# The last token group of a fused attention and expert kernel: 12 of 20 blocks take their first product from seven half-size products

## The chip, the core and the metric

The kernel runs on one core of a Trainium2 chip. The core has a matrix engine (TensorE, PE in the profile; PEld is its weight loads), a vector engine (VectorE, DVE), a scalar engine (ScalarE, ACT), GpSimd (POOL), SyncE (SP), and DMA engines that move data between the device memory and the core's own memory. The engines run side by side, each in the order of its own instructions, and wait for each other through semaphores. Matmul results land in PSUM, a small memory of banks of 512 numbers in each of 128 partitions. The metric is the device time of one execution in microseconds (us); lower is better.

## The reference

A sketched polynomial attention makes `x` (4352 tokens of 128 numbers); a routing then balances a matrix `P` of token and expert weights in eight rounds; eight experts with one hidden layer of 1024 each are summed with these weights:

```python
    logits = x @ w_gate
    logits = logits - logits.max()
    P = np.exp(logits)
    for _ in range(8):
        P /= P.sum(1, keepdims=True) + 1e-09
        P /= P.sum(0, keepdims=True) + 1e-09
        P *= N / E
    for e in range(E):
        h = np.maximum(x @ w1[e], 0.0)
        ye = h @ w2[e]
        out += P[:, e:e + 1] * ye
```

N is 4352, D 128, E 8 and F 1024, all float32.

## The kernel before, in words

Tokens lie along the free dimension, so a first product takes 128 features in and gives 128 hidden units out for some hundred tokens. A list `groups` (line 767) cuts the work into groups of tokens with the experts that each of them meets; an item is a group with one expert, and a block is a part of an item's hidden units.

- Nine plain groups without routing weights run in and between the attention and the routing, since they don't need `P`. Function `steps` (line 1654) yields their blocks in pieces, and `fill` (line 1746) drops these pieces between the statements of `attention` (line 635) and of `routing` (line 702). `passed` counts the pieces, and `aside` holds other small jobs that are due at a count of pieces.
- Five groups of three times 256 tokens follow (`middle`, line 1330). There both products are formed from fewer products of half or quarter size, at the price of sums on DVE, ACT and by accumulating DMAs. The matrix engine is addressed there as four tiles of 64 rows by 64 columns, which run at once. The order of every instruction is written out by hand (`SEAM`, `DRAIN` and the like).
- The last group has 2 times 256 tokens and the experts 3 to 7: five items of four blocks, 20 blocks in all, again out of `steps`. I number them 0 to 19. The first steps of blocks 0 to 2 are already issued inside `middle`. In a block, four steps each form 128 hidden units for 256 tokens (`first`, line 1173: two matmuls side by side, each on all 128 rows and one half of the columns, then a relu on ACT). The second product is formed from seven half-size products instead of eight (`seven`, line 1260; two side by side again), for which `two` (line 1187) makes sums of the hidden units on DVE, and `sums_of_two` (line 193) makes four sums of the parts of W2 for each expert, each 128 x 256, on DVE, in the last group itself. Second products stand `LAG` = 8 steps behind their first products.
- Both kinds of items need x times the routing weight: `prepare_x` (line 864) loads a broadcast row of `P` (tile `px`), `weigh_by_vector` (line 809) multiplies it by x. In the five middle groups `weigh_half` (880), `copy_half` (893) and `join_halves` (900) make the sums of x: a scaled half, a copy of it, and four accumulating DMAs on POOL's queue, of which the third reads what the first two wrote.
- In the routing every round has a reduction over experts (line 731), one over tokens (line 738), a pair of small matmuls that add over partitions (line 742) and the scaling of both (lines 735 and 748). DVE does all but the matmuls; these stand at a fixed place in PE's order, so PE waits there if DVE is late.
- During the same time `forms_ahead` (line 276) makes the first weights' sums for the experts 1 to 7 with DMAs on SP's and POOL's queues and sign changes on ACT (line 295), and stores them in device memory; `forms_of_five` (line 626) sets when.

The matrix engine works on float32 in two passes, so each matmul of the program shows as two records in the trace.

Of the kernel before, what the change touches and what calls it, by code (L numbers as in the profile page):

```python
# [44 lines left out]
def kernel(  # L45
# [12 lines left out]
    nc = tc.nc  # L58
# [558 lines left out]
    def forms_at(e, area, *steps_):  # L617
        for at_, do in zip(steps_, forms_ahead(e, area)):
            aside.setdefault(passed[0] + at_, []).append(do)

    def forms_of_two():
        kx = pieces(ld.tile([P, SA, D], F32, tag="k", name="kx", bufs=1), 2)
# [79 lines left out]
    def routing():  # L702

        forms_of_five()
        yield 6
        logits(0)
        logits(1)
        yield 0.5
        logits_turned()
        logits(2)  # L710
        yield 0.5
        logits_turned()
        logits_turned()
# [12 lines left out]

        step = 1.5 * 2.0 ** (23 - 149 + 64)
        nc.vector.tensor_scalar(pw[:, :, 0:E], pw[:, :, 0:E], step, step, op0=Alu.add, op1=Alu.subtract)
        for it in range(ITERS):
            rs = sk.tile([P, SA], F32, tag="rs", name="rs")  # L730
            nc.vector.reduce_sum(rs, pw, axis=AX.X)
            nc.vector.reciprocal(rs, rs)
            yield 1.25
            p1 = p1s[it % 2]
            nc.vector.scalar_tensor_tensor(p1[:, 0:SA], rs.unsqueeze(2).to_broadcast([P, SA, E]), UP,
                                           pw[:, :, 0:E], op0=Alu.mult, op1=Alu.mult)
            cs = sk.tile([P, E], F32, tag="cs", name="cs")
            nc.vector.reduce_sum(cs, p1.rearrange("p g e -> p e g"), axis=AX.X)
            yield 3
            pc = bank()[:, 0:E]  # L740
            for s in range(2):
                nc.tensor.matmul(pc[64 * s:64 * (s + 1)], ones[:, 0:64], cs, start=True, stop=True,  # L742
                                 tile_position=(0, 64 * s))
            cr = sk.tile([P, E], F32, tag="cr", name="cr")
            nc.vector.reciprocal(cr, pc)
# [382 lines left out]

    blocks = [(j, q) for j in range(len(items)) for q in range(FO // (4 if tiles_of(j) == 3 else 2))]
    LAG, given = 8, []

    HELD = 8
    hs = {}

    def room_of(k):

        lo, n, t, _, weighted = groups[items[blocks[k][0]][0]]
        if t == 3:  # L1140
            if "x" not in hs:
                hs["x"] = pools[0].tile([P, 25, NT3], F32, name="hx", bufs=1)
            return hs["x"] if k % 2 == 0 else hb[:, 0:25 * NT3].rearrange("p (b n) -> p b n", n=NT3)
        base = hs["x"].rearrange("p b n -> p (b n)") if weighted else hb
        size = 4 * (NT3 if weighted else 480)
        one, other = (13 * NT3 + size * (k % 3), size * (k % 2)) if weighted else (size * (k % 3), size * (3 + k % 2))

        m = k - held_blocks[0]
# [38 lines left out]
    def two(k):  # L1187
# [5 lines left out]
        def step(c):  # L1193
            if k == 0:
                c = 2 * (c % 2) + c // 2
            f, t = 2 * q + c // 2, c % 2
            first(k, f, t * n, (t + 1) * n, h[c], k % 2)

        def less(out, a, b):
# [60 lines left out]
    def seven(k):  # L1260
# [2 lines left out]
        _, w2, ws = loaded_w[j]  # L1263
        h, ts, _ = hs[k]
        lo, hi = slice(0, H2), slice(H2, DM)
        p1 = (w2[:, 2 * q, lo], h[0], 0, 0, 0)

        five, six = (0, 2) if weighted_of(k) else (2, 0)
        p6 = (ws[:, 1, q], ts[2], six, 1, 0)
        p2 = (w2[:, 2 * q + 1, lo], h[2], 1, 0, 0)  # L1270
        p4 = (w2[:, 2 * q + 1, hi], ts[3], 1, 1, 0)
# [382 lines left out]
    def steps():  # L1654
# [13 lines left out]
        for k in ks:  # L1668
            if k in news:
                if k == news[0]:  # L1670
                    while todo or sums_at:
                        between(t)
                        t += 1
                    phase.append(True)
                    yield 0
                    middle()
                    yield 0
                continue
            if k == len(blocks):
                for i, ps in enumerate(last_products()):  # L1680
                    todo.setdefault(t + i, []).extend(ps)
            if k < len(blocks):
# [25 lines left out]
                m, step, sums_ = ready.get(k) or two(k)  # L1708
                products = eight if g in DIRECT else seven
            for c in range(m if k < len(blocks) else 4):  # L1710
                if k < len(blocks) and k not in ready:
                    step(c)
                between(t)
                if k < len(blocks) and first_new - 2 <= j < first_new:
                    for do, *a in TAIL.get(16 * (j - first_new + 2) + 4 * q + c, ()):
# [3 lines left out]
                if k < len(blocks) and c == 0:  # L1719
# [2 lines left out]
                            sums_at.setdefault(t + i, []).append(lambda i=i, f=sums_: f(i))  # L1722
                    if k < len(blocks) - 2 and k not in held_blocks:
                        for i, ps in enumerate(products(k)):
                            todo.setdefault(t + LAG + i, []).extend((k, p) for p in ps)
                share = n / 480 * (16 / 15 if g in DIRECT else 1)
                if k >= len(blocks):
                    while later:
                        later.pop(0)()
                elif later and (c % 2 or share > 0.9 or c and weighted):  # L1730
                    later.pop(0)()
                if k not in ready:
                    yield share
# [119 lines left out]
```

## Time and profile before

| | |
|---|---|
| runs | 882.81 us (median of 3; 882.0 to 884.62) |
| the profiled execution's own time | 883.17 us |
| its span on the core | 881.4 us |
| granted TensorE clock | 0.999 of full speed |
| PE busy / DVE busy / ACT busy | 874.2 / 790.9 / 570.6 us |

The profile's page lists for each engine how long it was busy, a map of the span in 40 slices, and the chain of work that ended last. Other views give the busy time of each engine in chosen stretches, the single instructions in order of time, the instructions grouped by line, and who waited for whom. In a row such as `64*64 64x256 f32` the first part is the rows and columns of the matrix engine that are active, and the second the moving operand. A busy PE is a modelled figure, since matmuls overlap; the distances between starts are measured.

### The profile page before, as it was taken

The numbers are of one execution on the slowest core, as the hardware profiler recorded it, in microseconds if no ns is written. First come the engines' busy times: TensorE is split into PE (matmuls) and PEld (weight loads), VectorE is DVE, ScalarE is ACT, GpSimd is POOL, SyncE is SP. The second block draws the span as 40 slices with busy tenths as digits, with TensorE's granted clock in tenths as the row PEclk, the third lists the DMA queues.
The fourth block names the chain that finished last, engine by engine and source line by source line (L and its number), as shares of the span: only waits on it lengthen the run. The fifth ranks groups of instructions, "written<-read, shape, count | busy, mean of one in ns | idle before, by whom it ended". The sixth has DMA issues, their size and how long they took to land.

```text
span 881.4 us, 28702 instructions
## 1 busy us (share of the span) xinstructions
PE 874.2 (99%) x11790; PEld 652.2 (74%) x11790; DVE 790.9 (90%) x1631; ACT 570.6 (65%) x1308; POOL 176.6 (20%) x244
## 2 busy tenths in 40 slices
PE   9999999999999999999999999999999999999997
PEld 6787567564777888887878778788777777776665
DVE  7679689888999999999999999999998999998875
ACT  3346578668676677667676766666766766665643
POOL 2131433121212121312132112221222122200000
PEclk9999999999999999999999999999999999999999
DMA  8999699575887887777786776697577777674340
GB/s 238 282 287 291 150 232 230 140 175 186 233 217 214 215 252 213 211 196 212 220 209 178 212 217 176 176 245 226 156 179 222 216 217 186 203 204 97 96 105 13
DMA packets 97459, 174.64 MB, mean 198 GB/s; under 512 B 29088, under 2 KB 68848, under 8 KB 92480
## 3 DMA queue, kind: packets, MB, share of 16 engines
q1 hardware_dynamic: 74904, 139.65, 50.1%
q0 software_dynamic: 21264, 33.00, 21.6%
q8 instruction: 93, 1.52, 0.7%
q10 hardware_dynamic: 1160, 0.15, 0.1%
q14 instruction: 38, 0.31, 0.1%
HBM read 125.67 MB, written 25.08 MB: 171 GB/s over the span
## 4 chain that ended last, share of the span: by engine, by line
PE 98%; DMA 1%; DVE 0%; ACT 0%; issue 0%; SPq 0%; DVEq 0%; ACTq 0%
PE s L1634 42%; PE a L1347 38%; PE a L1179 14%; PE a L430 1%; PE a L556 1%; DMA qx<-in_q_dram 1%; PE s L462 0%; PE a L397 0%; PE a L520 0%; PE s L482 0%; PE a L482 0%; ACT hb L1183 0%; PE a L742 0%; SPq L156 0%; PE a L597 0%
## 5 line engine op out<-in xcount | busy, mean ns | idle before, releaser
L1347 PE MATMUL a<-xe,w 64*64 64x384 f32 x2164 | 417.2, 483 | 0.0
L1634 PE MATMUL s<-hb,ws 64*64 64x256 f32 (+4 forms) x2962 | 382.6, 384 | 0.0
L1634 PE MATMUL s<-hx,ws 64*64 64x256 f32 (+1 forms) x2894 | 348.9, 376 | 0.0
L1347 PE MATMUL a<-de,w 64*64 64x384 f32 x1600 | 307.3, 483 | 0.0
L1634 PEld LDWEIGHTS s<-hb,ws 64*64 64x64 f32 (+1 forms) x2962 | 203.5, 133 | 62.7 <-issue 16.6
L1634 PEld LDWEIGHTS s<-hx,ws 64*64 64x64 f32 (+1 forms) x2894 | 196.2, 133 | 55.2 <-issue 12.5
L1249 DVE TENSOR_TENSOR hb<-hb 128x512 f32<-128x512 f32 (+1 forms) x340 | 187.4, 576 | 1.4 <-ACT hb L1382 1.1
L1347 PEld LDWEIGHTS a<-xe,w 64*64 64x64 f32 x2164 | 145.7, 133 | 18.6 <-issue 1.1
L1382 ACT ACTIVATE hx<-a 128x384 f32<-128x384 f32 x204 | 97.0, 492 | 63.0 <-PE a L1347 61.5
L1382 ACT ACTIVATE hb<-a 128x384 f32<-128x384 f32 x204 | 97.7, 492 | 58.9 <-PE a L1347 57.5
L1179 PE MATMUL a<-xT,w 128*64 128x256 f32 (+3 forms) x576 | 129.8, 454 | 0.1
L1347 PEld LDWEIGHTS a<-de,w 64*64 64x64 f32 x1600 | 110.6, 133 | 17.3 <-ACT hb L1382 0.6
L1249 DVE TENSOR_TENSOR hx<-hx 128x512 f32<-128x512 f32 (+1 forms) x204 | 118.1, 594 | 0.0
L905 POOL DMA_DIRECT2D de<-xe x68 | 57.1, 989 | 295.2 <-ACT de L898 175.3
L1183 ACT ACTIVATE hb<-a 128x256 f32<-128x256 f32 (+3 forms) x148 | 66.9, 454 | 54.8 <-PE a L1179 49.3
L1378 ACT ACTIVATE hb<-a 128x384 f32<-128x384 f32 x136 | 66.7, 491 | 32.7 <-PE a L1347 31.8
L1387 DVE TENSOR_TENSOR a<-a,hb 128x384 f32<-128x384 f32 x136 | 76.6, 563 | 10.0 <-PE a L1347 5.9
L1376 ACT COPY a<-a 128x384 f32<-128x384 f32 x136 | 63.0, 464 | 32.5 <-PE a L1347 31.9
L1179 PEld LDWEIGHTS a<-xT,w 128*64 128x64 f32 x576 | 57.9, 137 | 24.2 <-issue 3.5
L1200 DVE TENSOR_TENSOR hb<-hb 128x416 f32<-128x416 f32 (+7 forms) x90 | 59.7, 664 | 14.4 <-ACT hb L1183 10.2
L1634 PE MATMUL s<-hb,w 128*64 128x256 f32 (+3 forms) x280 | 68.8, 434 | 0.0
L905 POOL DMA_DIRECT2D de<-de x34 | 29.7, 872 | 131.3 <-issue 74.3
(227 smaller groups left out, 1016.9 us busy)
## 6 DMA issues: line engine op xcount, KB each, us to landing
ws<-ws SPq DMA_DIRECT2D x34, 1280.0 KB, 6.6
w<-wl SPq DMA_DIRECT2D x34, 512.0 KB, 8.0
w<-wf SPq DMA_DIRECT2D x33, 512.0 KB, 8.6
px<-pT SPq DMA_DIRECT2D x34, 384.0 KB, 9.5
w<-in_moe_w_dram SPq DMA_DIRECT2D x16, 512.0 KB, 4.3
de<-xe POOLq DMA_DIRECT2D x34, 192.0 KB, 3.2
de<-de POOLq DMA_DIRECT2D x34, 192.0 KB, 8.2
ws<-in_moe_w_dram SPq DMA_DIRECT2D x7, 512.0 KB, 7.6
```

Source lines behind the costliest of these rows:

```text
L430: nc.tensor.matmul(pv[64 * s:64 * (s + 1), i], kp[0:n, H * t + h].rearrange("p i j -> p (i j)"), vx[0:n, slots[h], t, :], start=(t == 0 an ...
L905: tc.keep_in_program_order(nc.gpsimd.dma_start(out=out, in_=x, accum_op=Alu.add))
L1179: nc.tensor.matmul(ph[sl], loaded_w[j][0][:, P * f + H2 * s:P * f + H2 * (s + 1)], sources[j][:, lo:hi], start=True, stop=True, tile_posit ...
L1183: last_relu[:] = [nc.scalar.activation(out=out, in_=ph, func=Act.Relu).ins.name]
L1200: nc.vector.tensor_tensor(out, a, b, op=Alu.subtract)
L1249: nc.vector.tensor_tensor(places(out), places(a), places(b), op=Alu.subtract if off else Alu.add)
L1347: nc.tensor.matmul(out[sl], w[r, c0 + H2 * s:c0 + H2 * (s + 1)], x[r], start=start, stop=stop, tile_position=(H2 * row, H2 * s), skip_grou ...
L1376: witness(k, p, 1, nc.scalar.copy(b, bx))
L1378: witness(k, p, 5, nc.scalar.activation(out=m5s[p], in_=b, func=Act.Copy, scale=1.0 if p else -1.0))
L1382: ins = nc.scalar.activation(out=out, in_=x, func=Act.Relu)
L1387: ins = nc.vector.tensor_tensor(by if what == 1 else raw(k, p, 1, 1), bb[p], m5s[p], op=Alu.add)
L1634: mm = nc.tensor.matmul(sums[g][i][H2 * s:H2 * (s + 1), n * place:n * (place + 1)], w, x, start=c == (2 if t == 3 and row is None else 1) ...
```

## The change

Blocks 6 to 17 of the last group (`MIXED`) no longer form their first product by four steps. They go in pairs, and for each of the two blocks seven half-size products stand in for it (`mixed_product`): each is two matmuls in tiles of 64 rows by 64 columns, so that four matmuls run at once. A pair takes seven slots (`mixed_slot`), and each slot also issues ACT's and DVE's work on the results: relus, a seeded copy (`seed`), a sign change (`turned_five`), sums (`plus_five`) and the sums for the second products. Products number 4 of a pair run in the first two slots of the next pair; after the last pair they run in two slots of their own beside block 18. Second products, which stay on all 128 rows, stand between the slots.

For these blocks x needs sums as in the middle groups: `mixed_weigh` or `mixed_turn`, `mixed_copy`, and `mixed_join` with its four accumulating DMAs, at the places that `AHEAD` sets. The items of the experts 4 to 7 load `W2`, both stored forms of `W1` and the stored sums of `W2`, and experts 4 and 7 `W1` as well (`mixed_weights`); before they loaded `W1` and `W2`.

The sums of `W2` for the experts 4 to 7 are no longer made in the last group but during the routing (`pairs_ahead`): for each a load of `W2` (512 KB, SP), four DVE sums and a store (512 KB, SP).

```diff
+    def sums_of_pairs(e, w2, ws):
+        def load():
+            tc.keep_in_program_order(nc.sync.dma_start(out=w2, in_=moe_w2[e].rearrange("(fo fi) d -> fi fo d", fi=P)))
...
+        def some(i):
+            o, a, b, op = sums_[i]
+            return lambda: nc.vector.tensor_tensor(o, a, b, op=op)
+        def keep_():
+            stored_pairs[e] = dram.tile([P, 4, FO // 2, H2], F32, name=f"ws2{e}")
+            tc.keep_in_program_order(nc.sync.dma_start(out=stored_pairs[e], in_=ws))
+        return load, *(some(i) for i in range(4)), keep_
+    def pairs_ahead():
...
+        for n, e in enumerate(range(4, E)):
+            at_ = passed[0] + 15 + 9 * n
+            for later_, do in zip((0, 6, 7, 7, 8, 8), sums_of_pairs(e, w2, ws)):
+                aside.setdefault(at_ + later_, []).append(do)
@@ routing @@
         forms_of_five()
+        pairs_ahead()
         yield 6
@@ prepare_w @@
+        elif j in mixed_items:
+            mixed_weights(j)
@@ new, beside two and seven @@
+    mixed_items = range(len(items) - 4, len(items))
+    MIXED = range(len(blocks) - 14, len(blocks) - 2)
+    def mixed_join(j):
+        xe, de = mixed_x[j]
+        for out, x in ((de[upper], xe[lower]), (de[lower, 1], xe[upper, 1]), (de[:, 0], de[:, 1]),
+                       (xe[lower, 1], xe[lower, 0])):
+            tc.keep_in_program_order(nc.gpsimd.dma_start(out=out, in_=x, accum_op=Alu.add))
+    def mixed_product(pair, p, n):
...
+        out, row, w, c0, x, start, stop = {
+            1: (bx, 0, wl, fa, xe[:, 0], not p, False), 2: (bx, 1, wl, fa, xe[:, 0], False, True),
+            3: (by, 1, wl, fb, de[:, 0], False, True), 4: (b, 1, wf, fb, xe[:, 1], False, True),
+            5: (by, p, wf, fa, de[:, 1], not p, True), 6: (b, 0, wf, fb, de[:, 0], False, True),
+            7: (b, 0, wl, fb, xe[:, 1], False, True)}[n]
+        for s in range(2):
+            sl = slice(H2 * s, H2 * (s + 1))
+            mm = nc.tensor.matmul(out[sl], w[r, c0 + H2 * s:c0 + H2 * (s + 1)], x[r], start=start, stop=stop,
+                                  tile_position=(H2 * row, H2 * s), skip_group_check=True)
...
+    ROW_SLOTS = (((0, 5), (0, 4)), ((0, 1), (1, 4)), ((1, 1), (1, 5)), ((0, 6), (0, 2)), ((1, 6), (1, 2)),
+                 ((0, 7), (0, 3)), ((1, 7), (1, 3)))
+    def mixed_slot(k, w):
...
+        for row, (p, n) in enumerate(ROW_SLOTS[w % 7] if w < 7 else ()):
+            pair = before if row and w < 2 else now
+            if pair:
+                mixed_product(pair, p, n)
...
+    AHEAD = {(2, 0): (fetch_x(J5),), (3, 0): (turn_to(J4, 0, 0),), (3, 1): (turn_to(J4, 0, 1),),
+             (3, 2): (turn_to(J4, 1, 0),), (3, 3): (turn_to(J4, 1, 1), join(J4)),
+             (5, 0): (weigh(J5, 0),), (5, 1): (copy_of(J5, 0),), (5, 2): (weigh(J5, 1),),
+             (5, 3): (copy_of(J5, 1), join(J5)), (6, 0): (fetch_x(J6),),
+             (8, 0): (fetch_x(J7), lambda: prepare_w(J6)), (8, 3): (weigh(J6, 0),), (8, 4): (weigh(J6, 1),),
+             (8, 5): (copy_of(J6, 0),), (8, 6): (copy_of(J6, 1), join(J6)),
...
+             (12, 4): (turn_to(J7, 1, 1), join(J7))}
@@ steps @@
+            if k in MIXED:
+                if (k - MIXED[0]) % 2:
+                    continue
+                for c in range(7):
+                    mixed_slot(k, c)
+                    if c == 0:
+                        ends = [seven(k + s) for s in range(2)]
...
+                        for i, ps in enumerate(ps if ps[5] else (*ps[:4], [], ps[4])):
+                            todo.setdefault(t + 10 + i, []).extend((k, p) for p in ps)
+                    ahead_of(k, c)
+                    between(t)
...
+                    t += 1
+                    yield 1
+                continue
...
+                tail = 4 * (k - len(blocks) + 2) + c
+                if 0 <= tail < 4:
+                    mixed_slot(None, tail)
```

The first number in a key of `AHEAD` is the block of the last group (0 to 19), the second the step or slot in it; J4 to J7 are the items of the experts 4 to 7.

More of the change, by code (lines that the diff above doesn't have):

```diff
@@ new lines, in mixed_rooms, with mixed_weigh @@
+    def mixed_rooms(j):
+        mixed_x[j] = [pools[0].tile([P, 2, HALF], F32, tag=tag, name=tag, bufs=3)[:, :, 0:NT3] for tag in ("xe", "de")]
+        return mixed_x[j]
+    def mixed_weigh(j, i):
+        xe = (mixed_x.get(j) or mixed_rooms(j))[0]
+        sl = slice(NT3 * i, NT3 * (i + 1))
+        x, pb = xT[:, groups[items[j][0]][0]:][:, sl], sources[j][:, sl]
+        if i:
+            nc.vector.scalar_tensor_tensor(xe[:, i], x, -1.0, pb, op0=Alu.mult, op1=Alu.mult)
+        else:
+            nc.vector.tensor_tensor(xe[:, i], x, pb, op=Alu.mult)
@@ new lines, with mixed_pair @@
+    m5_rooms = [hb[:, NT3 * (32 + p):NT3 * (33 + p)] for p in range(2)]
+    side, beside = [], {}
+    def mixed_pair(k):
+        if not beside:
+            a, b = ([t[:, NT3 * p:NT3 * (p + 1)] for p in range(2)] for t in (bank(), bank()))
+            beside["bx"], beside["by"] = [b[0], a[1]], [a[0], b[1]]
+            beside["b"] = [bank()[:, 0:NT3] for _ in range(2)]
+        i = (k - MIXED[0]) // 2 % 2
+        h = hb[:, NT3 * (16 + 8 * i):NT3 * (24 + 8 * i)].rearrange("p (a b n) -> p a b n", a=2, b=4)
+        t = hs["x"][:, 8 * i:8 * (i + 1)].rearrange("p (a b) n -> p a b n", a=2)
+        hv, tv = ([x[:, :, c] for c in range(4)] for x in (h, t))
+        if k >= len(blocks) - HELD:
+            x = hb[:, 2 * NT3 * (k - len(blocks) + HELD):][:, 0:4 * NT3].rearrange("p (a b n) -> p a b n", a=2, b=2)
+            hv[2], tv[3] = x[:, :, 0], x[:, :, 1]
+        for s in range(2):
+            hs[k + s] = ([x[:, s] for x in hv], [x[:, s] for x in tv], (h[:, s, 1::2], h[:, s, 0:2], t[:, s, 0:2]))
+        return k, hv, tv
@@ new lines, in mixed_product @@
+    def mixed_product(pair, p, n):
+        k = pair[0] + p
+        j, q = blocks[k]
+        (wl, wf), (xe, de) = mixed_w[j], mixed_x[j]
+        fa = P * (4 * (q // 2) + p)
+        fb = fa + 2 * P
+        bx, by, b = (beside[x][p] for x in ("bx", "by", "b"))
+        out, row, w, c0, x, start, stop = {
[3 more added lines that the diff above has]
+            7: (b, 0, wl, fb, xe[:, 1], False, True)}[n]
+        r = (lower, upper)[row]
+        for s in range(2):
+            sl = slice(H2 * s, H2 * (s + 1))
+            mm = nc.tensor.matmul(out[sl], w[r, c0 + H2 * s:c0 + H2 * (s + 1)], x[r], start=start, stop=stop,
+                                  tile_position=(H2 * row, H2 * s), skip_group_check=True)
+            if not s and (n, p) in ((1, 0), (5, 1)) and (n, p) in seen_by:
+                tc.add_manual_dep(mm.ins, seen_by.pop((n, p)), SYNC, reason="row tiles of one bank")
@@ L1134, with ahead_of @@
+    def ahead_of(k, c):
+        for do in AHEAD.get((k - len(blocks) + 20, c), ()):
+            do()
     HELD = 8
@@ L1146, in room_of @@
         one, other = (13 * NT3 + size * (k % 3), size * (k % 2)) if weighted else (size * (k % 3), size * (3 + k % 2))
+        if k >= len(blocks) - 2:
+            one = 16 * NT3 + size * (k % 2)
         m = k - held_blocks[0]
@@ L1729, in steps @@
                         later.pop(0)()
-                elif later and (c % 2 or share > 0.9 or c and weighted):
+                elif later and (c % 2 or share > 0.9 or weighted and (c or k > len(blocks) - 20)):
                     later.pop(0)()
```

138 lines of the change are left out of this document (132 added, 6 removed).

## The prediction

> **What bounds the kernel now.** I read the page first: busy times, then the chain of work that ended last.
>
> ```profile
> span 881.4 us, 28702 instructions
> ...
> PE 874.2 (99%) x11790; PEld 652.2 (74%) x11790; DVE 790.9 (90%) x1631; ACT 570.6 (65%) x1308; POOL 176.6 (20%) x244
> ...
> PE 98%; DMA 1%; DVE 0%; ACT 0%; issue 0%; SPq 0%; DVEq 0%; ACTq 0%
> ```
>
> PE works 874.2 of 881.4 us and carries 98% of the chain. A PE slot saved anywhere shortens the end, and any stop of PE lengthens it. So I ask three things: how many slots the change saves, what it costs PE to run the new slots, and where PE comes to wait that didn't before.
>
> Second, the timeline of PE in the last group (start, duration, engine, line, operation, count), at the seam between the middle and the last group, where both kinds of slots already alternate:
>
> ```profile
> 807.27 1.95 PE L1179 MATMUL a<-px,w 128*64 128x256 f32 x16
> 809.15 2.39 PE L1634 MATMUL s<-hb,ws 64*64 64x256 f32 x40
> 811.47 1.95 PE L1179 MATMUL a<-px,w 128*64 128x256 f32 x16
> 813.35 1.51 PE L1634 MATMUL s<-hb,ws 64*64 64x256 f32 x20
> 814.79 1.95 PE L1179 MATMUL a<-px,w 128*64 128x256 f32 x16
> ...
> 820.46 0.38 PE L1179 MATMUL a<-px,w 128*64 128x256 f32 x1
> ...
> 821.32 0.60 PE L1179 MATMUL a<-px,w 128*64 128x256 f32 x4
> ...
> 827.79 0.60 PE L1179 MATMUL a<-px,w 128*64 128x256 f32 x4
> ```
>
> *The slot.* From 821.32 to 827.79 run two plain blocks of the last group: 6.47 us. A block has four first steps and three and a half second-product slots (seven half products, two side by side), so two blocks are 15 slots and a slot is 6.47 / 15 = 0.431 us. On 128 rows a slot is four records, on 64-row tiles eight.
>
> *The change of tiles.* From 807.27 to 811.47 stand four slots on 128 rows (16 records) and five on 64 rows (40 records): 9 x 0.431 = 3.88 us, but 4.20 went by: 0.32 us more for one change to 64-row tiles and one back. From 811.47 to 814.79 it is four and two and a half (20 records; its last slot is half filled and takes a whole one, so 7 x 0.431 = 3.02): 3.32 went by, 0.30 more. A there-and-back costs 0.30 to 0.32 us; I use 0.31.
>
> Third, the weight loads at the same place, to see what the time is spent on:
>
> ```profile
> 807.27 1.49 PEld L1179 LDWEIGHTS a<-px,w 128*64 128x64 f32 x16 [0.39 <-issue]
> 809.15 1.93 PEld L1634 LDWEIGHTS s<-hb,ws 64*64 64x64 f32 x40 [0.38 <-ACT hx L1183]
> ```
>
> One is put down to ACT, the other to nothing that can be waited for ("issue"), with the same 0.38 to 0.39 us of gap. So I take the price to belong to the change of tiles.
>
> **The change: products.** Twelve blocks have 48 first-step slots. Six pairs take 7 slots each and the drain 2: 44. Saved 4 x 0.431 = 1.73 us. At two places an odd half of a second product now runs alone and wastes half a slot, +0.43. Net -1.3 us.
>
> **The change: tiles.** Between the mixed slots stand second products on 128 rows. In PE's new order 36 runs of 64-row matmuls, in the six pairs and the two drain slots, each lie between runs of 128 rows. 36 x 0.31 = +11.2 us (10.8 to 11.5 by the two rows). Nothing hides it, because PE itself is the bound. Last group so far: +9.9.
>
> The Trainium skill, page "TensorEngine Tiling (Array Packing)", section Tiling Modes, Key Properties, says that a change of the tiling mode, as against a change of the tile, drains TensorE. It gives no price; the 0.30 to 0.32 us of the rows agrees, and by that rule all 36 are paid however early the operands are. The same page's Theoretical Speedup table speaks of gain alone, by which the sum would be -1.3 here; the rows speak against that.
>
> **The change: ACT and DVE in the mixed slots.** A pair lasts 14 slots and about six changes there and back, 6.0 + 1.9 = 7.9 us.
>
> ```profile
> L1183 ACT ACTIVATE hx<-a 128x256 f32<-128x256 f32 x64 | 24.2, 384 | 21.8 <-PE a L1179 18.4 <-PE s L1634 2.5
> ...
> L201 DVE TENSOR_TENSOR ws<-w 128x256 f32<-128x256 f32 x8 | 3.3, 418 | 2.0 <-DMA w<-in_moe_w_dram 2.0
> ...
> L1029 DVE TENSOR_TENSOR m<-s,x 128x256 f32<-128x256 f32 x1 | 0.4, 424 | 0.1
> ```
>
> These are groups of instructions of the last 65 us (count, busy us, mean ns, idle before). ACT has some 12 operations of 384 ns for a pair, 4.6 us; DVE some 10 or 11 of 0.42, 4.5 us. Both fit in 7.9 us, so I charge nothing. If they didn't, PE would wait in each slot for a bank.
>
> **The change: joins.** The DMA view gives the accumulating transfers (KB each, median us from issue to landing):
>
> ```profile
> de<-xe POOLq DMA_DIRECT2D x34, 192.0 KB, 3.2
> de<-de POOLq DMA_DIRECT2D x34, 192.0 KB, 8.2
> ...
> ws<-in_moe_w_dram SPq DMA_DIRECT2D x7, 512.0 KB, 7.6
> ...
> xe<-xe POOLq DMA_DIRECT2D x34, 96.0 KB, 9.0
> ```
>
> The join of item J4 is issued with block 3's last step. That step's first matmul is the row at 820.46; with relu and sign turn on ACT (0.38 each) and the queue the first transfer starts near 822, it and the second land by 826 (3.2 and some), and the third, which reads both, 8.2 later: 834.5. If the third takes no longer than the first, 829.5. Product 6 of block 6 needs it. Block 6 starts where it did, at 827.79, and product 6 stands six slots on (counting second products between) behind two there-and-backs: 827.79 + 2.6 + 0.6 = 831.0. Late by 3.5 or early by 1.5; between the ends I take 1.5. The joins of J5, J6 and J7 need some 12.5 us by the same rows (about 4 for the first two, 8.2, issue); a pair and the way to its product 6 (7.9 + 3.2) leave 11 to 12.6 at each: 0 to 1.6, and a late one moves the need for the next back as well; I take 0.5 for the three. Weight loads (2 MB for each of J5 to J7, against 1 MB before) share the DMA engines, whose share there is 0.37 to 0.43 in the stretches below. Joins together: **+2**, from 0 to 6.
>
> ```profile
> 816.00:838.00 22.00, 22.00 (x208) 14.64 (x206) 19.75 (x46) 12.97 (x35) 1.73 (x2) 1.00 0.37 97
> 838.00:860.00 22.00, 22.00 (x208) 14.64 (x206) 15.53 (x36) 10.81 (x29) 0.00 (x0) 1.00 0.43 103
> ```
>
> (Columns: stretch, sum, PE, PEld, DVE, ACT, POOL busy with counts, granted clock, DMA share, GB/s.)
>
> **The change: sums in the routing.** What is taken away from the last group's DVE (16 sums, 6.7 us at 418 ns) lay under PE and is worth nothing there. The routing is the same kind of view, over 132 to 172 us:
>
> ```profile
> 132.00:154.00 22.00, 22.00 (x141) 16.35 (x139) 20.02 (x39) 18.92 (x40) 7.28 (x8) 1.00 1.02 230
> 154.00:172.00 18.00, 17.88 (x122) 10.51 (x120) 16.75 (x32) 10.54 (x22) 1.72 (x2) 1.00 0.59 148
> ```
>
> DVE is full and so are the DMA engines. PE waits for DVE once a round (L742 behind the reduction at L738). The timeline, DVE and PE together:
>
> ```profile
> 126.72 2.26 DVE L1200 TENSOR_TENSOR hb<-hb 128x832 f32<-128x832 f32 x3
> 129.49 0.21 DVE L745 RECIPROCAL cr<-a 128x8 f32<-128x8 f32 x1 [0.51 <-PE a L742]
> 136.25 1.02 DVE L1200 TENSOR_TENSOR hb<-hb 128x832 f32<-128x832 f32 x1 [1.12 <-ACT hb L1183]
> 147.56 0.66 DVE L738 TENSOR_REDUCE cs<-p 128x8 f32<-128x280 f32 x1
> 161.13 0.66 DVE L738 TENSOR_REDUCE cs<-p 128x8 f32<-128x280 f32 x1
> ```
>
> ```profile
> 148.95 0.23 PE L742 MATMUL a<-cs,ones 128*64 128x8 f32 x2
> 161.94 0.29 PE L742 MATMUL a<-cs,ones 128*64 128x8 f32 x4
> ```
>
> In the round at 147.56 the reduction ends at 148.22 and PE uses it at 148.95: 0.73 us. In the round at 161.13 it ends at 161.79 and PE takes it 0.15 later: bare handover, no margin. So the first of these has 0.58 to spare, the second none. In DVE's new order 8 of the 16 sums stand ahead of the first and 12 ahead of the second. DVE idles 0.51 and 1.12 us on the way (the two brackets), which sums can fill. At the first: 8 x 0.42 - 1.63 - 0.58 = 1.15 us late; at the second 12 x 0.42 - 1.63 = 3.4 us, the first included. Sums behind it meet the spare time of the later round.
>
> That is with W2 there in time. The first load stands on SP's queue behind these:
>
> ```profile
> 121.93 2.52 SPq L292 DMA_DIRECT2D rb<-in_moe_w_dram  x3
> ...
> rb<-in_moe_w_dram SPq DMA_DIRECT2D x2, 256.0 KB, 7.6
> ```
>
> It is issued near 124.5, and the first sum stands at 128.98 (126.72 + 2.26), where DVE began the 0.51 us of idle time. At the 7.6 us that 256 KB took here, or the 7.6 of 512 KB elsewhere, it lands after 132: DVE stands for 3.5 us more, queued ahead of that round's scaling (L745). Stores on SP wait for the last sum, and behind them the forms' loads of later experts, on which ACT's sign changes (L295) depend. So 3.4 + 3.5 = 6.9: I take **+7**. Ends: above 10 (a second load late, by 1 us, and 2 for SP's queue); below, if the load is early and all DVE's idle time of the two stretches (1.98 + 1.25) is used instead of 1.12 of it, 3.4 - 2.1 = 1.3.
>
> The Trainium skill, "DMA: Bandwidth & Descriptors", section on the anatomy of one DMA, fits 2.0 us plus the bytes over 436 GB/s; an estimate by it for 512 KB is 3.2 us. The load would be there before 128.98, and the routing would cost 3.4. The rows have 7.6 us; they decide.
>
> **Sum.** -1.3 + 11.2 + 2 + 7 = +18.9 us. The profiled execution took 883.17 (span 881.4 and 1.8 around it): 902.1. The median of the runs, 882.81, is 0.4 below it: 901.7, said as 901.5.
>
> **Rivals.**
> - *Not slower.* What costs 0.31 is not the change of tiles but late operands: the row at 809.15 names ACT. In the mixed slots operands are some slots early, so nothing would be lost, and the products' gain of 1.3 stands. With the routing at its lower end (+1.3) and joins in time this gives 881.5 to 882.8. It decides only if a there-and-back costs under 0.04 us (1.3 / 36). Against it: the row at 807.27, same gap, no one to wait for. 6%.
> - *Routing absorbed.* 9.9 + 1.3 + 1 (joins): about 894.5. For it: ACT and PE have spare time in the rounds. Against: DVE 20.02 of 22. 17%.
> - *Changes free, the rest paid.* -1.3 + 2 + 7: 890.5. 5%.
> - *Joins late at every item*, transfers at 8 to 9 us under the doubled weight loads: joins 6, routing 10: 9.9 + 16 = 908.7. 15%.
> - *The change doesn't do what it says*, the weaving lost because PE's order is other than the slots': its order shows the slots, so 2%, near 883.
>
> **How the numbers follow.** Forecast 55%: 898 to 905. From "routing absorbed" to the middle of "joins late": 892 to 910 leaves out the first rival, the third and a part of the fourth, about two in ten. 0.3% (2.6 us) is what a measurement here can tell from no change: faster 0.03, same 0.04, slower 0.93.
>
> **What would show it.** In the new trace: 64-row runs of the last group with about 0.15 us of gap beyond a slot at either side, whoever the releaser; twelve mixed blocks taking about 10 us more than before; PE waiting for L738 near 149 and 162 and DVE for a W2 load near 129; the last group starting some 7 us later; product 6 of block 6 waiting for a DMA. It is wrong if the changes inside the group cost under 0.2 us there and back, or the last group starts at its old time.

## The result and the profile after

The changed kernel takes 906.5 us (median of 6 runs, 905.61 to 907.25), the kernel before 883.41 (6 runs, 882.0 to 884.62): a ratio of 1.0262, 95% interval 1.0249 to 1.0275. The forecast was 901.5, range 892 to 910. The page of the changed kernel, its own span, busy times and chain of work that ended last:

```profile
span 904.7 us, 29095 instructions
...
PE 890.5 (98%) x11934; PEld 631.9 (70%) x11934; DVE 797.8 (88%) x1645; ACT 580.4 (64%) x1344; POOL 190.8 (21%) x260
...
PE 90%; DMA 4%; DVE 3%; issue 1%; ACT 1%; SPq 0%; POOL 0%; DVEq 0%; POOLq 0%; ACTq 0%
```

PE carried 98% of the chain before and 90% now; DMA, DVE and ACT have 8% between them. To place the 23.3 us (904.7 - 881.4) I compared when the same matmul starts in both traces, at a place ahead of the new work and at one behind the routing. PE's timeline in the kernel before:

```profile
98.08 0.57 PE L1634 MATMUL s<-hb,ws 128*64 128x416 f32 x2
...
207.44 0.38 PE L1634 MATMUL s<-hb,ws 128*64 128x256 f32 x1
```

and in the changed kernel:

```profile
96.64 0.57 PE L1888 MATMUL s<-hb,ws 128*64 128x416 f32 x2
...
214.50 0.38 PE L1888 MATMUL s<-hb,ws 128*64 128x256 f32 x1
```

The changed kernel was 1.44 us ahead at the first and 7.06 behind at the second: 8.50 lost in and around the routing. From there to the start of the last group the distance stays 7.06. The last group accounts for the other 16.2 (23.3 - 7.06).

**The routing.** DVE's timeline of the changed kernel shows the place:

```profile
124.82 2.27 DVE L1453 TENSOR_TENSOR hb<-hb 128x832 f32<-128x832 f32 x3
133.26 0.42 DVE L636 TENSOR_TENSOR ph<-kx 128x256 f32<-128x256 f32 x1 [6.17 <-DMA wl<-in_moe_w_dram]
```

At the first of W2's sums (L636) DVE stands 6.17 us. The row names a load into `wl`, but the sum reads `kx`. In the view of the transfers issued between 124.5 and 125.5 us (KB each, us from issue to landing) that load of W2 stands as

```profile
kx<-in_moe_w_dram SPq DMA_DIRECT2D x1, 512.0 KB, 8.2
```

Issued at 124.94 (SP's queue, below), it landed at 133.1, when DVE went on; the named load only landed last before it. PE's timeline shows who waits for DVE:

```profile
132.37 0.86 PE L1888 MATMUL s<-hb,ws 128*64 128x416 f32 x2
133.86 0.92 PE L1432 MATMUL a<-xT,w 128*64 128x416 f32 x4 [0.62 <-DVE cr L780]
134.60 0.86 PE L1888 MATMUL s<-hb,w 128*64 128x416 f32 x2
138.32 0.96 PE L1888 MATMUL s<-hb,ws 128*64 128x416 f32 x1 [2.86 <-DVE hb L1453]
```

SP's queue, in order of issue:

```profile
124.94 0.62 SPq L626 DMA_DIRECT2D kx<-in_moe_w_dram  x1
...
127.91 2.10 SPq L292 DMA_DIRECT2D ph<-in_moe_w_dram  x3
139.76 0.35 SPq L640 DMA_DIRECT2D ws<-ph  x1
140.22 0.55 SPq L292 DMA_DIRECT2D wl<-v  x1
```

SP itself stands from 130.0 to 139.76, because the store (L640) waits for the fourth sum, and the forms' transfers stand behind the store.

**The last group.** PE's timeline over one pair of mixed blocks (L1273 are the half-size products):

```profile
854.38 0.43 PE L1273 MATMUL a<-xe,ws 64*64 64x256 f32 x2
...
854.66 0.80 PE L1273 MATMUL a<-de,ws 64*64 64x256 f32 x6
855.84 0.65 PE L1273 MATMUL a<-xe,ws 64*64 64x256 f32 x4 [0.38 <-ACT hb L1312]
856.42 0.43 PE L1888 MATMUL s<-hb,kept 128*64 128x256 f32 x1
...
863.32 0.43 PE L1273 MATMUL a<-xe,ws 64*64 64x256 f32 x2
```

A pair lasts 8.93 us (854.38 to 863.32, by the unrounded starts). Its 14 slots make 6.04 and its six changes of tiles there and back 1.86, together 7.90; 1.03 is left. It is all at one place: the pair's third and fourth slots stand side by side there, with no second product between them. Of the six records from 854.66 two end product 5 of the third slot and four are product 6 of the fourth, alone; product 2, which should run beside product 6, starts only at 855.84. ACT's timeline:

```profile
855.13 0.36 ACT L1316 COPY a<-a 128x256 f32<-128x256 f32 x1 [0.95 <-PE a L1273]
855.40 0.39 ACT L1312 ACTIVATE hb<-a 128x256 f32<-128x256 f32 x1
```

The turn of product 5 (L1312) ends at 855.79, and PE's weight load goes 0.05 us later. Product 2 doesn't read the turned product, but its bank is the one that the turn reads the other half of. So product 6 and product 2 run one behind the other, with 0.55 us of waiting between them. PE's waits in the last group (in total, times, longest) are these six, one in each pair, and no others; the kernel before has none there:

```profile
PE a L1273 <- ACT hb L1312: 2.3, 6, 0.4
```

The wait is for a semaphore of ACT, so it is an order that the program sets; no run here shows whether the chip needs it.

### The profile page after: what moved, and what is told of

The parts are those of the page before. It is cut to its first block, busy times and chain, and to the rows that moved or that the text cites. A ratio compares the mean times of both kernels' runs of the same rounds, so it can differ in the third digit from the quotient of the medians.

```text
span 904.7 us, 29095 instructions
## 1 busy us (share of the span) xinstructions
PE 890.5 (98%) x11934; PEld 631.9 (70%) x11934; DVE 797.8 (88%) x1645; ACT 580.4 (64%) x1344; POOL 190.8 (21%) x260
## 4 chain that ended last, share of the span: by engine, by line
PE 90%; DMA 4%; DVE 3%; issue 1%; ACT 1%; SPq 0%; POOL 0%; DVEq 0%; POOLq 0%; ACTq 0%
PE s L1888 39%; PE a L1601 37%; PE a L1432 7%; PE a L1273 3%; DMA ph<-in_moe_w_dram 2%; DVE hb L1453 1%; PE a L430 1%; DMA wl<-in_moe_w_dram 1%; DMA kx<-v 1%; PE a L556 1%; DMA pT<-qT 1%; DMA px<-pT 0%; PE a L397 0%; DVE ph L636 0%; PE s L462 0%
## 5 line engine op out<-in xcount | busy, mean ns | idle before, releaser
L1888 PE MATMUL s<-hb,ws 64*64 64x256 f32 (+4 forms) x2978 | 388.0, 384 | 3.6 <-DVE hb L1453 3.5
L1888 PE MATMUL s<-hx,ws 64*64 64x256 f32 (+1 forms) x2846 | 339.1, 377 | 0.0
L1888 PEld LDWEIGHTS s<-hb,ws 64*64 64x64 f32 (+1 forms) x2978 | 204.1, 133 | 74.2 <-issue 23.1
L1888 PEld LDWEIGHTS s<-hx,ws 64*64 64x64 f32 (+1 forms) x2846 | 188.7, 133 | 56.9 <-issue 15.0
L1436 ACT ACTIVATE hb<-a 128x256 f32<-128x256 f32 (+3 forms) x142 | 64.0, 456 | 54.4 <-PE a L1432 47.6
L1888 PE MATMUL s<-hb,w 128*64 128x256 f32 (+3 forms) x300 | 75.8, 435 | 0.0
L1432 PEld LDWEIGHTS a<-xT,w 128*64 128x64 f32 x576 | 54.0, 138 | 30.4 <-issue 13.2
```

What stands on the lines that cost most here:

```text
L1432: nc.tensor.matmul(ph[sl], loaded_w[j][0][:, P * f + H2 * s:P * f + H2 * (s + 1)], sources[j][:, lo:hi], start=True, stop=True, tile_posit ...
L1436: last_relu[:] = [nc.scalar.activation(out=out, in_=ph, func=Act.Relu).ins.name]
L1888: mm = nc.tensor.matmul(sums[g][i][H2 * s:H2 * (s + 1), n * place:n * (place + 1)], w, x, start=c == (2 if t == 3 and row is None else 1) ...
```

## The experiments

Lag is the start of the matmul at 207.44 in the kernel before, taken against the same matmul in the run, less the lag of the matmul at 98.08; it prices the routing part. The last group is the span less 881.4 less the lag at 207.44 (for sums_on_gpsimd the 15.25 at 800 us). All from profiled executions.

| kernel | median us | span | lag at 98, at 207 | routing part | last group |
|---|---|---|---|---|---|
| changed | 906.5 | 904.7 | -1.44, 7.06 | 8.50 | 16.2 |
| no_sums_in_routing | 898.79 | 896.6 | -1.03, -1.16 | -0.13 | 16.4 |
| routing_sums_only | 901.65 | 901.8 | -0.10, 4.00 | 4.10 | 16.4 |
| routing_transfers_only | 902.98 | 900.6 | 0.05, 2.94 | 2.89 | 16.3 |
| first_sums_later | 907.66 | 904.3 | -0.58, 6.67 | 7.25 | 16.2 |
| sums_on_gpsimd | 915.05 | 912.9 | -0.40, 15.10 | 15.50 | 16.2 |
| halved_rows_in_before | 892.2 | 889.5 | -1.11, -1.50 | -0.39 | 9.6 |
| second_products_later | 906.46 | 904.2 | -0.34, 6.81 | 7.15 | 16.0 |
| turned_first | 905.54 | 903.4 | -0.75, 7.44 | 8.19 | 14.6 |
| fewer_changes | 906.39 | 904.3 | -0.19, 9.40 | 9.59 | 13.5 |
| seven_lists | 905.97 | 903.9 | -0.97, 7.59 | 8.56 | 14.9 |
| lists_and_turn | 903.06 | 901.4 | -0.66, 6.42 | 7.08 | 13.6 |

**no_sums_in_routing**: is the routing part what the sums and their transfers cost?

```diff
-        pairs_ahead()
...
-        fetch(ws, stored_pairs[e])
+        fetch(ws.rearrange("p i q d -> p (i q d)"), moe_w1[e])
```

> The changed kernel without the four loads, sixteen sums and four stores in the routing; the last group loads other data of the same size (W1) in the place of the sums, so its second products are not the reference's. In the changed kernel PE fell back by 8.8 us between 121 and 198 us of the span against the kernel before (from 1.7 ahead to 7.1 behind). Theory (the routing part is paid in full): that disappears, about 897.5 to 898, still 14 to 15 slower than before, all of it in the last group. Rival (part of the 8.8 is a shift that the sums don't cause, as the 1.7 us ahead at the opening): the last group starts 3 or more us late all the same, 901 or above.

898.79 us, ratio 1.0179 (1.0164 to 1.0194). The routing part is -0.13 us, so the 8.50 belongs to these instructions. The rival falls. The last group keeps its 16.4.

**routing_sums_only** and **routing_transfers_only**: the two halves of the step.

```diff
-        w2 = rooms_ahead[0].rearrange("p a d -> p (a d)")[:, 0:F].rearrange("p (f d) -> p f d", f=FO)
+        w2 = xT[:, 0:F].rearrange("p (f d) -> p f d", f=FO)
...
+            for i, (later_, do) in enumerate(zip((0, 6, 7, 7, 8, 8), sums_of_pairs(e, w2, ws))):
+                if i not in (0, 5):
+                    aside.setdefault(at_ + later_, []).append(do)
```

```diff
+            for i, (later_, do) in enumerate(zip((0, 6, 7, 7, 8, 8), sums_of_pairs(e, w2, ws))):
+                if i in (0, 5):
+                    aside.setdefault(at_ + later_, []).append(do)
```

The first diff is the sums alone, the second the transfers alone; i counts the load, the four sums and the store. Both also load W1 in the place of the stored sums, as no_sums_in_routing does.

> The changed kernel with the sixteen DVE sums at their places in the routing, but without the loads and stores; the sums read x, which is there, and the last group loads W1 in their place, so the output isn't the reference's. Theory (the prediction's 3.4 us for DVE's work without late loads): 898.8 + 3.4 = 902.2, PE 3 to 4 us later behind the routing than in no_sums_in_routing. Rival (DVE has room for 6.7 us of sums, only the loads' lateness costs): within 1 us of 898.8. Rival (DVE's work is the whole cost): 905 or above.

> The changed kernel with the four loads of W2 and the four stores in the routing, but without the sixteen DVE sums between them; the stores keep what lies in the room, and the last group loads W1 in the place of the sums as in no_sums_in_routing (898.8 us, against 906.5 of the changed kernel), so the output isn't the reference's. The stores no longer wait for DVE, nor DVE for the loads. Theory (what costs is DVE's queue: its work and its standing at a late load): within 1 us of 898.8. Rival (4 MB more on full DMA engines and on SP's queue delay the forms' transfers and, through ACT, PE): 902 or above.

In the profiled executions DVE's sums alone cost 4.10 us and the transfers alone 2.89. By the medians it is the other way round: 901.65 for the sums is 2.86 above no_sums_in_routing, and 902.98 for the transfers 4.19. The profiled execution of routing_sums_only was the slowest of its four (903.59, the others 901.42 to 901.67), so the split between the halves is known to 1.3 us or so. That the sums cost something less than the whole, as expected, holds either way. So does the time of the transfers' rival, which the theory had at nothing, but not the way that it gave (through the forms and ACT): with no sum waiting for a load, DVE's waits in that run, from 180 us on, have

```profile
DVE xe L929 <- DMA px<-pT: 4.8, 1, 4.8
```

where DVE in the kernel before has no wait for `px` at all: the middle's first load of the routing weights comes late. Between 183 and 195 us of before's span this run fell back by 2.33 us. So the routing part can have a second place, at its end, which I had not looked at. In the changed kernel PE lost 0.79 us there.

**first_sums_later**: only the first late load.

```diff
-            at_ = passed[0] + 15 + 9 * n
-            for later_, do in zip((0, 6, 7, 7, 8, 8), sums_of_pairs(e, w2, ws)):
+            at_ = passed[0] + 15 + 9 * n + (2 if n else 0)
+            for later_, do in zip((0, 6, 7, 7, 8, 8) if n else (0, 9, 10, 10, 11, 11), sums_of_pairs(e, w2, ws)):
```

> The changed kernel with the first expert's four sums three pieces later than its load (the other experts two pieces later throughout). Theory (the 6.2 us for which DVE stands at the first sum is the load's lateness, and it is the larger part of the routing's cost): DVE's wait for the load falls under 1 us, the last group starts about 3.4 us late and not 7 to 8.8, and the time is 901 to 902. Rival (the DVE work of the sums is what costs, or the DMA engines are so full that the wait only moves): the time stays within 1.5 us of 906.5.

The wait at the first sum went, and another took its place at the third expert's load (DVE's timeline):

```profile
161.39 0.42 DVE L636 TENSOR_TENSOR ph<-kx 128x256 f32<-128x256 f32 x1 [3.81 <-DMA kx<-in_moe_w_dram]
```

The routing part is 7.25 (from the fastest of four executions, 906.11), the time 907.66. My theory that about 3.4 us are left without this wait falls. The changed kernel does lose most of its routing part at the first load (6.37 us, below), but loads, sums and stores are one chain through SP and DVE, and moving its first link moves the wait.

**sums_on_gpsimd**: DVE relieved.

```diff
-            return lambda: nc.vector.tensor_tensor(o, a, b, op=op)
+            return lambda: tc.keep_in_program_order(nc.gpsimd.tensor_tensor(o, a, b, op=op))
```

> The changed kernel with the sixteen sums of the routing on GpSimd (0.74 us each in the kernel before, at other sums of this size) and not on DVE, loads and stores as they are. Between 98 and 207 us of the span PE fell back by 7.2 to 9.6 us with all of it, by 4.1 with DVE's sums alone and by 2.9 with the transfers alone. Theory (DVE's queue carries the larger part): PE falls back by about 2.9 us only, 900 to 902. Rival (GpSimd then stands at the late loads, its own transfers of the forms with it, and ACT and PE wait for those): 7 us or more, 905 or above.

915.05 us, far on the rival's side. Sums and waits on POOL now stand ahead of the transfers of `P` at the routing's end, and the middle's first product with weights waits for them (DVE's timeline):

```profile
198.00 0.56 DVE L928 TENSOR_TENSOR xe<-xT,px 128x384 f32<-128x384 f32 x1 [8.94 <-DMA px<-pT]
```

**halved_rows_in_before**: the price of a change of tiles by itself.

```diff
+        r = lower if len(blocks) - 14 <= k < len(blocks) - 2 and lo == 0 else slice(0, P)
         for s in (1, 0) if flip else (0, 1):
             sl = slice(H2 * s, H2 * (s + 1))
-            nc.tensor.matmul(ph[sl], loaded_w[j][0][:, P * f + H2 * s:P * f + H2 * (s + 1)],
-                             sources[j][:, lo:hi], start=True, stop=True, tile_position=(0, H2 * s))
+            nc.tensor.matmul(ph[sl], loaded_w[j][0][r, P * f + H2 * s:P * f + H2 * (s + 1)],
+                             sources[j][r, lo:hi], start=True, stop=True, tile_position=(0, H2 * s))
```

> The kernel before, in which 24 of the last group's first steps (two of each of blocks 6 to 17) use only the lower 64 rows: the same number of matmuls and columns, no operand later than before, but 24 runs of 64-row matmuls, each between matmuls on 128 rows. The other half of the features is left out of these steps, so the output isn't the reference's. Theory (a change of tiles there and back costs 0.31 us whatever the operands): +7.4 us, 890.5 to 891. Rival (the 0.31 us belongs to late operands or their waits): within 1 us of before.

892.2 us, ratio 1.0103 (1.0088 to 1.0118); the last group is 9.6 us longer. PE's timeline of this run:

```profile
826.40 0.65 PE L1180 MATMUL a<-px,w 64*64 64x256 f32 x4
...
829.48 0.60 PE L1180 MATMUL a<-px,w 128*64 128x256 f32 x4
829.92 0.59 PE L1635 MATMUL s<-hx,ws 128*64 128x256 f32 x2
830.44 0.65 PE L1180 MATMUL a<-px,w 64*64 64x256 f32 x4
```

From 826.40 to 830.44 runs one block with two 64-row steps: 4.04 us. Its 7.5 slots make 3.24 and two changes there and back 0.62, together 3.86. The other 0.18 is at 829.92: there the odd half of the second product (two records, one column half) runs alone, and the change behind it keeps the other half idle, where before the next step slid in beside it. So 24 x 0.31 = 7.4 holds, with 2.2 us of odd halves more. No operand was later than before, so the rival (late operands) falls. By the Trainium skill ("TensorEngine Tiling (Array Packing)", Tiling Modes, Key Properties) a change of mode drains TensorE; this run agrees, with 0.31 us there and back.

**second_products_later**, **turned_first**, **seven_lists**, **lists_and_turn**: the 1.03 us that the sum had missed.

```diff
-                            todo.setdefault(t + 10 + i, []).extend((k, p) for p in ps)
+                            todo.setdefault(t + 11 + i, []).extend((k, p) for p in ps)
```

> The changed kernel with the lists of second products one slot later, so that the two slots of a pair between which none stands are the fourth and fifth and not the third and fourth. The number of changes of tiles is the same but for one (35 runs and not 36). In the changed kernel PE stops once in every pair, at product 2 of the first block, until ACT has turned product 5 of the second; with the half slot that is wasted there it is some 1.0 us a pair. Theory (the wait comes from two slots standing next to each other): it goes, six pairs give 5 to 6 us, about 901. Rival (the pair's chain of ACT and PE is as long as the slots, so the wait only moves to another slot): within 1.5 us of 906.5.

16.0 in the place of 16.2: the theory falls as put. Now the fourth and fifth slots stand side by side, and product 2 of the second block waits there, with the half slots one behind the other as before, for DVE's sum into the other half of its bank. PE's waits of this run in the last group:

```profile
PE a L1273 <- ACT hb L1312: 0.8, 2, 0.4
PE a L1273 <- DVE a L1322: 0.7, 4, 0.2
```

(In total, times, longest.) The wait moved to the next pair of neighbours.

```diff
-            seed(1)
-            turned_five(1)
+            turned_five(1)
+            seed(1)
```

> The changed kernel, in which ACT turns product 5 of a pair's second block before it copies the seed of that block, and not after it (third slot of a pair). In the changed kernel PE's load for product 2 of the first block goes on 0.05 us after the end of the turn. Theory (PE waits for that turn, though it reads the other half of the bank): each pair 0.27 us shorter (8.93 to 8.66 us), 1.6 us in all. Rival (it waits for the seed, which comes last now): each pair as long as before.

The last group is 1.6 us shorter, as expected (905.54 is the median of two runs). PE's timeline gives 854.15 - 845.51 = 8.64 us a pair:

```profile
845.51 0.43 PE L1273 MATMUL a<-xe,ws 64*64 64x256 f32 x2
...
854.15 0.43 PE L1273 MATMUL a<-xe,ws 64*64 64x256 f32 x2
```

So the wait is for the turn, whichever half of the bank it reads.

```diff
-                        for i, ps in enumerate(ps if ps[5] else (*ps[:4], [], ps[4])):
+                        for i, ps in enumerate((*ps[:5], ends[0][1], ends[1][1]) if ps[5] else (*ps[:4], [], ps[4])):
```

> The changed kernel with the last list of second products of a pair (four products, two slots) split into two lists for the pairs of blocks 6, 8 and 10, so that in three of the six pairs every slot is followed by second products and the third and fourth stand apart: 39 runs of 64-row matmuls in the place of 36. In the changed kernel such a pair lasts 8.93 us, where 14 slots and six changes there and back make 7.90. Theory (the other 1.03 us comes from the two slots standing next to each other: 0.55 us of waiting for ACT's turn, and two half slots that run one behind the other): the pairs with split lists last about 8.2 us (7.90 + 0.31), the others 8.9; the last group is 2.2 us shorter. Rival (the chain of ACT and DVE through a pair's banks is the limit, wherever the lists stand, as it was in second_products_later): the split pairs last 8.7 us or more.

With second products behind every slot a pair lasts 8.50 us (854.47 to 862.98, unrounded), between the two expectations. The split lists run in the pair behind their own, so the first such pair is the third:

```profile
854.47 0.43 PE L1273 MATMUL a<-xe,ws 64*64 64x256 f32 x2
...
855.65 0.65 PE L1273 MATMUL a<-de,ws 64*64 64x256 f32 x4
855.93 0.65 PE L1273 MATMUL a<-xe,ws 64*64 64x256 f32 x4
...
862.98 0.43 PE L1273 MATMUL a<-xe,ws 64*64 64x256 f32 x2
```

One more slot of distance is not quite enough: product 2 (855.93) starts 0.28 us behind product 6 (855.65), and 14 slots, seven changes there and back and this make 6.04 + 2.17 + 0.28 = 8.49. That left one guess to try, both edits together:

> The changed kernel with both edits, the split lists of seven_lists and the turn before the seed of turned_first. By the traces, a split pair lasted 8.50 us (14 slots and seven changes there and back make 8.21; product 2 still started 0.28 us behind its neighbour), and the swap gave 0.30 us a pair. Theory (what is left over 8.21 is the end of ACT's turn, which the swap moves forward): split pairs 8.21 us, the others 8.64; the last group 13.2 us longer than before's, about 903 to 904 with a routing part of 8. Rival (something else in the pair holds product 2): split pairs stay at 8.5 us.

```profile
852.72 0.43 PE L1273 MATMUL a<-xe,ws 64*64 64x256 f32 x2
...
855.07 0.43 PE L1273 MATMUL a<-de,ws 64*64 64x256 f32 x2
855.15 0.43 PE L1273 MATMUL a<-xe,ws 64*64 64x256 f32 x2
...
861.01 0.43 PE L1273 MATMUL a<-xe,ws 64*64 64x256 f32 x2
```

The same pair lasts 8.29 us: 8.21 for slots and changes, and product 2 still starts 0.08 behind product 6. So nearly all of what was left was the turn. The last group came to 13.6 against 13.2 expected, the time to 903.06.

**fewer_changes**: the lists two at a time.

```diff
-                            todo.setdefault(t + 10 + i, []).extend((k, p) for p in ps)
+                            todo.setdefault(t + 10 + (i // 2) * 2 + 1, []).extend((k, p) for p in ps)
```

> The changed kernel with the lists of second products issued two at a time: 23 runs of 64-row matmuls in the mixed part and not 36. Theory (changes of tiles at 0.31 us each way and back, and besides waits wherever two 64-row slots stand together, of about 1.0 us as at the one such place now): 13 x 0.31 = 4.0 us less, but two more places in each pair where slots stand together, up to 12 x 1.0 us more: 904 to 914, slower rather than faster than 906.5. Rival (changes alone matter): 902.5.

The last group is 2.7 us shorter: 4.0 for 13 changes saved, 1.3 given back. The median stayed at 906.39 all the same; in the profiled execution the routing part was 9.59. The high price that I expected of each new neighbourhood didn't come. PE's timeline:

```profile
848.57 0.43 PE L1273 MATMUL a<-xe,ws 64*64 64x256 f32 x2
...
850.03 0.43 PE L1273 MATMUL a<-xe,ws 64*64 64x256 f32 x2 [0.38 <-ACT hb L1312]
...
856.76 0.43 PE L1273 MATMUL a<-xe,ws 64*64 64x256 f32 x2
```

This pair is 8.19 us, the two behind it 8.0; 14 slots and three changes make 6.97. PE's waits in the mixed part name the turn, and beside it one wait of 0.7 us for a plain relu:

```profile
PE a L1273 <- ACT hb L1312: 2.2, 6, 0.4
```

None of these versions comes near the kernel before: even lists_and_turn is 2.35% slower (1.0218 to 1.0253).

## Why the prediction came out as it did

The range held, and the forecast of 901.5 was 5.0 us short. Term by term:

- *Products, -1.3, and changes of tiles, +11.2*: right. All 36 changes stand in the new trace at 0.31 there and back; halved_rows_in_before priced them without any of the rest. Products, changes and the missed wait make -1.3 + 11.2 + 6 x 1.03 = 16.1, against 16.2 measured.
- *"Both fit in 7.9 us, so I charge nothing"* (ACT and DVE in the mixed slots): this is the step that failed. I compared busy time with the length of a pair and didn't follow a single slot's chain: product 5, ACT's copy and turn, product 2 in the same bank. Where two slots are neighbours the chain is longer than the slot. It cost 1.03 us a pair, 6.2 in all. The text had named the form that it would take (a wait for a bank in a slot), without a price.
- *Joins, +2*: nothing. The new trace's joins on POOL's queue land sooner than the rows of the middle:

```profile
de<-xe POOLq DMA_DIRECT2D x4, 128.0 KB, 4.2
de<-de POOLq DMA_DIRECT2D x4, 128.0 KB, 2.7
```

 The third transfer took 2.7 us where I had 3.2 to 8.2. The first join's third transfer is issued at 833.87 and so lands near 836.6; product 6 of block 6 comes with these rows:

```profile
833.87 0.87 POOL L1236 DMA_DIRECT2D de<-de  x1 [2.16 <-DMA de<-xe]
```

```profile
837.98 0.80 PE L1273 MATMUL a<-de,ws 64*64 64x256 f32 x6
```

 Product 6 starts within this row, at 838.18: the predicted 831.0 and the 7.06 of lag, to about a tenth, and no wait is recorded there. The early end of my bounds (early by 1.5) was the true one.
- *Routing, +7 (3.4 for DVE's work, 3.5 for the late load)*: right in its mechanism. It was 8.50 in the profiled execution and 7.1 to 9.6 over those with all of it on DVE; the medians' difference of 23.1 us leaves 6.9 beside the 16.2 of the last group. PE's lag at four more matmuls (named by their starts in the kernel before) shows where it arises:

| kernel | lag at 130.02 | 139.79 | 164.01 | 192.34 |
|---|---|---|---|---|
| changed | -1.83 | 4.54 | 6.27 | 7.06 |
| second_products_later | -0.73 | 3.46 | 6.81 | 6.81 |
| turned_first | -0.84 | 3.32 | 6.67 | 7.44 |
| lists_and_turn | -1.05 | 3.07 | 6.42 | 6.42 |

 The first step is the stand at the load, the second the two rounds to which I gave DVE's work. In the last three kernels, whose granted clock stayed at 1.00 in this stretch, the steps are 4.1 to 4.2 and 3.35, for 3.5 and 3.4 in the sum; routing_sums_only, which has no loads, fell back by 3.3 over the second (0.67 at 139.91, 3.99 at 164.01). In the changed kernel the first is 6.37, with a lower clock behind it (last section), and the second 1.73. The third step, about 0.8 in the two of these where it occurs, is the late `px`, which I had not foreseen. The load took 8.2 us where I had 7.6; the fit that I set beside it from the Trainium skill ("DMA: Bandwidth & Descriptors", Anatomy of one DMA) is given there for GpSimd's path, and this load went by SP's queue.
- *The rivals*: "not slower" needed a there-and-back under 0.04 us and fell with halved_rows_in_before, as did "changes free"; "routing absorbed" fell with no_sums_in_routing, 7.7 us (906.5 - 898.79) under the changed kernel; joins were late at no item. (The sum for "routing absorbed" gives 895.0, not 894.5, and item J7 loads 2.5 MB, not 2; neither changes the outcome.)

Two errors of opposite sign made the sum look better than its parts, which was luck: joins 2 too much, the wait 6.2 too little. Not tried: banks of their own for the four half-bank sums, which would show the wait without any reordering, and the sums of W2 left in the last group, which would show whether the routing part has to be paid at all.

## What to carry to other kernels

On an engine that bounds the time, count the changes of mode that a new order makes before the operations that it saves: four slots saved (1.7 us) were paid for with 36 changes (11.2 us). Busy shares don't show a chain: follow one result from the matmul through the other engines to the matmul that needs its bank, where slots stand closest. A load, its use and its store through one in-order queue are one chain, and moving its first link moves the wait.

## What the runs showed that was not expected

After PE's stop of 2.9 us in the routing its matmuls ran slowly for some 3 us. Three stretches of the changed kernel (sum, engines, granted clock, DMA share, GB/s):

```profile
132.00:136.00 4.00, 2.85 (x12) 0.75 (x8) 2.64 (x7) 3.92 (x10) 0.88 (x1) 1.00 1.13 296
136.00:140.00 4.00, 1.68 (x10) 0.97 (x12) 3.93 (x10) 1.55 (x3) 0.00 (x0) 0.79 0.64 112
138.30:141.70 3.40, 3.38 (x14) 1.67 (x16) 3.37 (x6) 0.03 (x1) 0.00 (x0) 0.50 0.37 142
```

The clock was 0.79 from 136 to 140 and 0.50 from 138.3 to 141.7, and a matmul of 128x416 lasted 0.96 us (the row at 138.32), against 0.51 ahead of the stop:

```profile
128.53 0.51 PE L1888 MATMUL s<-hb,ws 128*64 128x416 f32 x1
```

 The Trainium skill, "TensorE: Matmul & The Clock Gate", Part 1, describes a gate that halves the clock of an array that has been idle until it has been busy for a few us; the row at 138.30 agrees. The page names an idle window of about 3.4 us, and here a stop of 2.86 us went ahead of it. A stop can so cost more than its length. But it need not: six of the profiles have a stop of 2.85 or 2.86 us at this place. In the changed kernel, seven_lists and fewer_changes the clock fell behind it (0.79, 0.50 and 0.61 from 140 to 144), and the routing parts were 8.50, 8.56 and 9.59; in lists_and_turn, second_products_later and turned_first it stayed at 1.00, and they were 7.08, 7.15 and 8.19. What decides whether the clock falls is not shown, and since the two sets lie close, neither is how much of the difference is the clock's.

The opening of the program, where the kernels are the same, differed from run to run by -1.44 to +0.05 us at 98 us; differences of that size between two profiles say nothing of an edit.
